# An attention step, a token sum and a first sum, each put at another place in a one-core kernel

## The chip, the cores and the metric

The kernel runs on one core of a Trainium2 chip. The metric is the time of one execution in microseconds (us), as the device measures it. The kernel before takes 810.32 us, the median of 3 runs (808.83 to 812.44).

The engines are named as in the profile: PE is TensorE (matmuls; PEld its weight loads), DVE is VectorE, ACT is ScalarE, POOL is GpSimd, and SP is SyncE, which issues most of the DMA transfers. Each works off its own queue in order. PE writes to PSUM, in banks that VectorE and ScalarE read out.

## The reference

Three layers follow each other. First an attention over 4 batches, 8 heads, 576 positions and 64 columns a head, in which the first four heads see a band of 32 positions and the others every fourth of 128:

```
scores = where(mask, scale * q @ k.T, -1e9)
attn   = softmax(scores)            # with 1e-9 added to the sum
x      = heads side by side of attn @ v      # 2304 tokens x 512
h = x @ w_in;  x2 = (h * sigmoid(h)) @ w_out         # 512 -> 2048 -> 512
a = x2 @ w1;  b = x2 @ w2;  out = ((a * b) @ w3) @ w_out2   # 512 -> 1024 -> 1024 -> 512
```

All is float32. The kernel splits each float32 factor into a high and a low part and does three matmuls for one (high x high, low x high, high x low).

## The kernel before, in words

The order of the work on each engine is written out by hand, under a manual schedule: code that is called earlier stands earlier in the queues of the engines it uses. Waits between engines come of themselves, from who reads and writes which buffer.

The 2304 tokens go through the second layer in five chunks; chunks 0, 1, 3 and 4 have 512 tokens, chunk 2 has 256. Attention for later chunks is done between the matmuls of earlier ones. A *slot* (c, f) belongs to chunk c and to the block f of 128 of the 2048 inner columns. In it PE does `h` for the next slot (12 matmuls) and `x` for this one (12 matmuls); ScalarE and VectorE turn h into g (`t`: tanh and a VectorE product, `g`: the high part on ScalarE and the low part on VectorE).

A slot's text in `SLOT` (L72) says what stands where: `h`, `H` are the halves of h, `x`, `X` those of x, `t` and `g` as above, `a` is the next attention step, and `p` is a token sum, if one is waiting. There is one text for a first slot of a pair and one for a second; `att.half()` picks it.

The attention goes two units at a time. A round has eight steps, as `ATT` (L71) lists them: V S (attention times v of the last round, scores of the next; PE), M (maxima, VectorE), E and E (exponentials, ScalarE), then in the second half N (sums on VectorE, products on GpSimd) with O (the output's high part on ScalarE and low part on VectorE), L (loads) with O, T (transposes on PE) and W (evacuation by ScalarE). T and V and S share two PSUM banks. In chunk 1 the rounds begin to lag behind the slot pairs: the limit on O holds a round back in slots 13 and 14.

The last two chunks do h by seven products of blocks in place of eight (`h_product`, L862, called in the loop at L1303). *Token sums* prepare the right-hand blocks: sums of the tokens' columns (`t_ops`), 6 early ones (x_a, x_b and a difference), 22 late ones (T1, T2, T4) and 4 last ones (T3). The late ones need tiles in the place of the attention's, so they start when the attention ends.

For the seven products there are eight rounds p. In round 0 the products go in the order 0, 2, 4, 1, 3, 5, 6, each into one of four banks in turn, and the two halves of x for the last slot of chunk 2 stand behind products 0 and 2. `collect_h` reads the banks: s1, u2, u3 and c22 hold the running sums, each finished one gets its tanh, product, high and low part. Between them, `sets` gives out single operations that prepare the third layer's weights (`set_ops`): a load of raw words, their conversion, sums and stores.

Of the kernel before, what the change touches and what calls it, by code (L numbers as in the profile page):

```python
# [9 lines left out]
F32R = mybir.dt.float32r  # L10
# [7 lines left out]
P = 128  # L18
# [53 lines left out]
SLOT = (  # L72
    ("ahapHppaxptapgX", "ahappHpxaptaXpg"),
    ("ahaHtapxgpaX", "ahHpaxtgpXaap"),
)
LATE_MICROS = 7
SET_AT = (1, 3, 6)
# [12 lines left out]
def tile_kernel(  # L90
# [338 lines left out]
    class Convert:  # L429
# [7 lines left out]
        def add(self, key, src, dst):  # L437
            self.todo.append((key, src, dst))
            return len(self.todo) - 1

        def load(self, i):
            if i < len(self.todo) and i not in self.raw:
                t = rawp.tile([P, 512, 2], I32, tag="raw", name=f"raw_{self.todo[i][0]}")
                nc.sync.dma_start(
                    out=t.rearrange("p n w -> p (n w)"), in_=self.todo[i][1].bitcast(I32)
                )
                self.raw[i] = t
# [406 lines left out]
    def load_sw(p, u):  # L854
        if p < NP and u == 0:
            dst = f32(wf[p + NP])[:, :1024].rearrange("p (s n) -> p s n", s=2)[:, :, :256]
            nc.sync.dma_start(out=dst, in_=swd[p][:, 0].rearrange("p (s k) -> p s k", s=2))
        elif p < NP:
            sw[u] = sp.tile([P, 512], F32R, tag=f"sw{u}", name=f"sw_{p}_{u}")
            nc.sync.dma_start(out=f32(sw[u]), in_=swd[p][:, u])  # L860
# [30 lines left out]
    def set_ops(s, t, raw, o):  # L891

        y = {}

        def load(k, i):
            if k < SETS:
                src = (w1, w2)[k % 2]
                nc.sync.dma_start(out=raw.rearrange("p n w -> p (n w)"), in_=src[k // 2 + i * NG // 2].bitcast(I32))

        def rebias(i):  # L900
            h = raw[:, :, 1].bitcast(F32)
            nc.scalar.activation(h, h, AF.Prelu, scale=2.0 ** -112, alpha=2.0 ** 32)

        def bits(i, x):
            if x == 0:
                y[i] = yp.tile([P, 512], I32, tag="y", name=f"ys_{s}_{i}")
                nc.vector.tensor_single_scalar(y[i], raw[:, :, 1], 3, op=ALU.logical_shift_left)
            else:
                nc.vector.scalar_tensor_tensor(
                    y[i], raw[:, :, 0], 29, y[i], op0=ALU.logical_shift_right, op1=ALU.bitwise_or  # L910
                )
                load(s + i, 1 - i)

        def half(i, k):
            return f32(y[i])[:, 256 * k:256 * k + 256]

        def total(u):
            if u == 0:
                nc.vector.tensor_add(t, half(1, 0), half(1, 1))
            elif u == 1:  # L920
                nc.vector.tensor_sub(t, t, half(0, 0))
            elif u == 3:
                nc.vector.tensor_sub(t, half(0, 1), t)
            else:
                nc.vector.tensor_sub(t, half(0, 0), half(1, 0))

        def high(k, x):
            nc.scalar.activation(o[:, k, 0].bitcast(F32R), x, AF.Copy)

        def low(k, x, at):  # L930
            nc.vector.tensor_sub(o[:, k, 1].bitcast(F32R), x, o[:, k, 0])
            nc.sync.dma_start(out=setd[s][:, at], in_=o[:, k].rearrange("p s k -> p (s k)"))

        def both(k, x, at):
            return [lambda: high(k % 2, x()), lambda: low(k % 2, x(), at)]

        def piece(i):
            return [lambda: rebias(i), lambda: bits(i, 0), lambda: bits(i, 1)]

        q = [lambda: load(0, 0)] if s == 0 else []  # L940
        q += piece(0)
        for h in range(2):
            q += both(h, lambda h=h: half(0, h), 4 + h)
        q += piece(1)
        for k, u in enumerate((0, 1, 3, 2)):
            q += [lambda u=u: total(u)] + both(k, lambda: t, u)
        return q + both(0, lambda: half(1, 1), 6)
# [187 lines left out]
    with tc.manual_schedule():  # L1135
# [49 lines left out]

        for i, (c, f) in list(enumerate(slots))[NF:-1]:
            nxt = slots[i + 1]
            for x in SLOT[c - 1][att.half()]:
                if x == "h":
                    if nxt[1] == 0:  # L1190
                        att.need(2)
                    h_part(*nxt, 0)
                elif x == "H":
                    h_part(*nxt, 1)
                    if nxt[1] == NF - 1:
                        att.limit = (c + 3) * PER_B
                elif x == "t":
                    g_tanh(*nxt)
                    g_mul(*nxt)
                elif x == "g":  # L1200
                    g_high(*nxt)
                    g_low(*nxt)
                elif x in "xX":
                    x2_part(c, f, "xX".index(x))
                    if x == "X" and f == NF - 1:
                        x2_store(c, (0, 2))
                elif x == "a":
                    if att.step() or c < 2:
                        pass
                    elif "T" in tmps:  # L1210
                        if todo:
                            todo.pop(0)()
                    else:
                        attn.close()
                        parts_ = ctx.enter_context(ExitStack())
                        sp = parts_.enter_context(tc.tile_pool(name="sp", bufs=1, side="right", reuse_waits="tile"))
                        tmps["T"] = [sp.tile([P, 2, 2, 512], F32R, tag=f"T{n}", name=f"T{n}") for n in range(2)]
                        for u in (1, 2, 3):
                            load_sw(0, u)
                        todo += late  # L1220
                elif x == "p" and todo and (len(todo) > len(early) or c == 2 and (att.out >= 3 * PER_B + 6 or "T" in tmps)):
                    todo.pop(0)()
        load_sw(0, 0)
# [3 lines left out]
        def gate(c):  # L1227
            nc.scalar.activation(ts[0], c, AF.Tanh, scale=0.5)
            return ts[0]

        def mul(c, t):
            nc.vector.scalar_tensor_tensor(c, t, 1.0, c, op0=ALU.add, op1=ALU.mult)
# [16 lines left out]
        def collect_h(p, i):  # L1249
# [29 lines left out]
            else:  # L1279
# [4 lines left out]
                split_high(ga[e], u3)  # L1284
                cs["t"] = gate(u2)

        def finish_h(p):
            u2, u3, e = cs["u2"], cs["u3"], p + NP
            mul(u2, cs["t"])
            split_low(ga[e], u3)  # L1290
            split_high(g_late(p), u2)
            split_low(g_late(p), u2)
# [10 lines left out]
        for p in range(NP):  # L1303
            if p == 1:
                bank = [ps_x.tile([P, 512], F32, tag="x", name=f"hx{k}") for k in range(4)]
                xps[3] = [(ps_h if m < 2 else ps_a).tile([P, 512], F32, tag="h" if m < 2 else "a", name=f"x2_3_{m}")
                          for m in range(KT)]
            for j, i in enumerate((0, 2, 4, 1, 3, 5, 6) if p == 0 else range(7)):
                live[i] = bank[done[0] % 4]
                done[0] += 1  # L1310
                h_product(p, i, live[i])
                if p == 0 and j < 2:
                    x2_part(2, NF - 1, j)
                    if j == 1:
                        x2_store(2, (0, 2))
                        raws = [rawp.tile([P, 2, 512], F32, tag="raw", name=f"c_{k}") for k in range(2)]
                        cs.update(s1=raws[0][:, 0], u2=raws[0][:, 1], u3=raws[1][:, 0], c22=raws[1][:, 1])
                        o = rawp.tile([P, 2, 2, 256], F32, tag="raw", name="set_out")
                        w = rawp.tile([P, 512, 2], I32, tag="raw", name="set_raw")
                        t = sp.tile([P, 256], F32, tag="set_t", name="set_t")  # L1320
                        sets = [op for s in range(SETS) for op in set_ops(s, t, w, o)]
                        ts.append(gp.tile([P, 512], F32, tag="t", name="t_s", bufs=1))
                        collect_h(0, 0)
                elif p == 0:
                    for k in {1: (1, 2), 3: (3, 4), 5: (5,), 6: (6,)}.get(i, ()):
                        collect_h(0, k)
                else:
                    collect_h(p, i)
                x_some(3, xs, 4 if i < 3 else 3, NF - 1)
                for _ in range(2 if i in (1, 2, 3, 5) else 1):  # L1330
                    if sets and (p or j > 2):
                        sets.pop(0)()
            xs = first_x(p)
        finish_h(NP - 1)
# [165 lines left out]
```

## Time and profile before

| | |
|---|---|
| median of 3 runs | 810.32 us (808.83 to 812.44) |
| the profiled execution | 808.31 us, span 806.5 us |
| PE busy | 787.4 us, 98% of the span |
| VectorE, ScalarE, GpSimd busy | 557.4, 346.6, 57.5 us |
| attention within chunks 0 to 2 | until 288 us |
| seven products | 309 to 431 us |

How to read it: the span is the time between the first and the last instruction that the profiler saw, and the profiled execution's own time is 1.8 us longer. Busy times of engines add up to more than the span, as they work side by side. Idle time counts where nobody else could have gone on: with PE at 98% that is PE's own idle time. The granted clock is given as a part of TensorE's full 2.4 GHz.

### The profile page before, as it was taken

How to read it: one execution, taken by the hardware profiler on the slowest of the kernel's cores; microseconds unless marked ns; L12 is line 12 of the kernel's file. 1: busy time of each engine (PE TensorE's matmuls, PEld its weight loads, DVE VectorE, ACT ScalarE, POOL GpSimd, SP SyncE). 2: the span in 40 equal slices, each digit the busy share in tenths (PEclk: the TensorE clock that was granted, in tenths of full speed). 3: DMA queues.
4: the chain of work that ended last, by engine and by line, in shares of the span. 5: the costliest groups of instructions: out<-in, count | busy, mean ns of one | idle time of the engine just before them, and what ended most of it. 6: DMA issues, size and time to landing. Idle time of an engine off the chain costs nothing. (4 is left out here: it accounts for less than half of the span.)

```text
span 806.5 us, 13326 instructions
## 1 busy us (share of the span) xinstructions
PE 787.4 (98%) x4829; PEld 680.7 (84%) x4829; DVE 557.4 (69%) x1333; ACT 346.6 (43%) x867; POOL 57.5 (7%) x90
## 2 busy tenths in 40 slices
PE   8999999999998899999999999999999999999997
PEld 7788888888887898788888888889999999999996
DVE  6989983867664564788884857778877655774444
ACT  7778873545444543444442625342333111321111
POOL 5101100101001100000000000013200000000000
PEclk9999999999999999999999999999999999999999
DMA  9788640533334103445532859627621760046202
GB/s 257 231 261 261 195 134 2 193 134 128 119 108 153 52 17 92 144 143 170 157 117 82 301 191 366 222 79 266 274 100 32 230 239 23 1 145 208 92 1 78
DMA packets 54561, 120.93 MB, mean 150 GB/s; under 512 B 5088, under 2 KB 25312, under 8 KB 52448
## 3 DMA queue, kind: packets, MB, share of 16 engines
q1 hardware_dynamic: 54208, 119.85, 44.3%
q8 instruction: 38, 0.62, 0.3%
q14 instruction: 27, 0.22, 0.1%
q10 hardware_dynamic: 288, 0.23, 0.1%
HBM read 87.56 MB, written 32.51 MB: 149 GB/s over the span
## 5 line engine op out<-in xcount | busy, mean ns | idle before, releaser
L1043 PE MATMUL bank<-xT,wf 128*128 128x384 f32 x864 | 163.7, 335 | 0.5 <-DVE wf L492 0.4
L1043 PEld LDWEIGHTS bank<-xT,wf 128*128 128x128 f32 x864 | 151.8, 188 | 7.2 <-DVE wf L492 0.9
L750 PE MATMUL x<-g,wf 128*128 128x512 f32 (+1 forms) x576 | 122.1, 357 | 0.7 <-ACT g L733 0.7
L710 PE MATMUL h<-xT,wf 128*128 128x512 f32 (+1 forms) x576 | 122.2, 361 | 0.0
L1099 PE MATMUL o<-wf,wf 128*128 128x512 f32 x429 | 110.0, 393 | 0.0
L710 PEld LDWEIGHTS h<-xT,wf 128*128 128x128 f32 x576 | 96.3, 192 | 15.7
L750 PEld LDWEIGHTS x<-g,wf 128*128 128x128 f32 x576 | 95.2, 189 | 16.2 <-ACT g L733 0.9
L1099 PEld LDWEIGHTS o<-wf,wf 128*128 128x128 f32 x429 | 79.5, 188 | 12.7
L1079 ACT ACTIVATE wf<-c 128x384 fp32r<-128x384 f32 x48 | 25.2, 525 | 84.0 <-DVE c L1077 83.8
L728 DVE SCALAR_TENSOR_TENSOR t<-t,h 128x512 f32<-128x512 f32 (+1 forms) x48 | 28.6, 597 | 42.4 <-ACT t L724 42.0
L1061 ACT ACTIVATE s<-bank 128x384 f32<-128x384 f32 x24 | 11.8, 492 | 103.4 <-PE bank L1043 92.8
L884 PE MATMUL x<-ga,wf 128*128 128x512 f32 x192 | 52.9, 396 | 1.9 <-DVE c L1280 1.9
L264 ACT ACTIVATE sm<-sm,nm 128x96 f32<-128x96 f32 x108 | 39.1, 365 | 23.6 <-DVE nm L254 23.5
L689 PE MATMUL wp<-wf,wf 128*128 128x512 f32 x192 | 46.7, 392 | 0.0
L884 PEld LDWEIGHTS x<-ga,wf 128*128 128x128 f32 x192 | 36.5, 191 | 10.5 <-DVE c L1280 2.3
L279 POOL TENSOR_TENSOR sm<-sm,rs 128x288 f32<-128x288 f32 x36 | 27.6, 779 | 229.8 <-DVE rs L274 63.9
L884 PE MATMUL x<-wf 128*128 128x512 f32 x192 | 43.7, 389 | 0.0
L1068 DVE TENSOR_TENSOR c<-u,bank 128x384 f32<-128x384 f32 x36 | 19.9, 552 | 32.8 <-PE bank L1043 32.6
L884 PEld LDWEIGHTS x<-wf 128*128 128x128 f32 x192 | 36.0, 188 | 7.5
L724 ACT ACTIVATE t<-h 128x512 f32<-128x512 f32 (+1 forms) x48 | 25.1, 522 | 39.0 <-PE h L710 35.6
L689 PEld LDWEIGHTS wp<-wf,wf 128*128 128x128 f32 x192 | 35.7, 188 | 7.2 <-DVE wf L605 0.4
L738 DVE TENSOR_TENSOR g<-t,g 128x512 fp32r<-128x512 f32 (+1 forms) x48 | 30.0, 626 | 15.6 <-ACT g L733 15.2
(167 smaller groups left out, 1215.1 us busy)
## 6 DMA issues: line engine op xcount, KB each, us to landing
rawj<-in_w_dram SPq DMA_DIRECT2D x26, 512.0 KB, 5.9
wf<-setd SPq DMA_DIRECT2D x11, 1024.0 KB, 5.4
wf<-setd SPq DMA_DIRECT2D x11, 768.0 KB, 7.2
raw_i<-in_w_in_dram SPq DMA_DIRECT2D x16, 512.0 KB, 4.6
raw_u<-in_w_out_dram SPq DMA_DIRECT2D x16, 512.0 KB, 4.4
swd<-sw SPq DMA_DIRECT2D x16, 512.0 KB, 2.6
sw<-swd SPq DMA_DIRECT2D x24, 256.0 KB, 3.2
setd<-set_out SPq DMA_DIRECT2D x21, 256.0 KB, 2.1
```

What stands on the lines that cost most here:

```text
L264: nc.scalar.activation(sm[:, j], sm[:, j], AF.Exp, bias=nm[:, j:j + 1], scale=-1.0, accum_out=su[:, j:j + 1],)
L279: nc.gpsimd.tensor_tensor(sm, sm, rs[:, :NB].to_broadcast([P, NB, KB]), op=ALU.mult)
L689: nc.tensor.matmul(wp_ps[i], a[:, i // 2, sa, i % 2 * P:(i % 2 + 1) * P], o[:, sb], start=(jt == 0 and x == 0), stop=(jt == NG - 1 and x = ...
L710: nc.tensor.matmul(ps, win(f, sa, kt), xT[:, kt, sb, r0:r0 + n], start=(kt == 0 and x == 0), stop=(kt == KT - 1 and x == 2),)
L724: nc.scalar.activation(gt[c, f], hps[c, f][:, :n], AF.Tanh, scale=0.5)
L728: nc.vector.scalar_tensor_tensor(t, t, 1.0, ps, op0=ALU.add, op1=ALU.mult)
L738: nc.vector.tensor_sub(g[:, 1], t, f32(g[:, 0]))
L750: nc.tensor.matmul(xps[c][m][:, :n], wout(f, sa, m), g[:, sb], start=(f == 0 and sa == 0 and sb == 0), stop=(f == NF - 1 and sb == 1),)
L884: nc.tensor.matmul(xps[c][m], wout(f, sa, m), g[:, sb], start=(first_ and sa == 0 and sb == 0), stop=(last and sb == 1),)
L1043: nc.tensor.matmul(b, a_op(s, a, sa, kt), b_op(x, sb, kt), start=(n == 0), stop=(n == 5),)
L1079: behind.append((count[0] + 1, lambda: nc.scalar.activation(hi, c[k], AF.Copy)))
L1099: nc.tensor.matmul(ps, g_block(jj, n, sa)[:, m % 3 * P:(m % 3 + 1) * P], wp_v(f, sb)[:, c0:c1], start=((first_ or len(parts) == 2) and x = ...
```

## The change

There are three edits.

One: at a slot's start the half is noted, and an `a` does a step only if the next step belongs to that half. A slot pair that has fallen out of step with the rounds then stays where it is until its half comes.

Two: once the attention has no steps left, tiles for the late token sums are taken at a slot's start, and a third text in `SLOT` is used, the same for both halves: five `p`, none of them between `t` and `g`.

Three: in round 0 of the seven products the sums are built in another order (`begin_h`): u2 = b0 + b4 and s1 = b0 + b2 after product 4, then u3 = b0 + b1 and u2 += b1, then c22 = u2 + b3 and u3 += b3, where s1 and u3 start as two copies of b0. No operation of a set is given out in round 0 any more, but the first load of raw words is issued there at once; later rounds give out 12 operations in place of 11.

```diff
 SLOT = (
     ("ahapHppaxptapgX", "ahappHpxaptaXpg"),
     ("ahaHtapxgpaX", "ahHpaxtgpXaap"),
+    ("phpHtxgpXpp",) * 2,
 )
...
-        q = [lambda: load(0, 0)] if s == 0 else []
-        q += piece(0)
+        if s == 0:
+            load(0, 0)
+        q = piece(0)
...
-            for x in SLOT[c - 1][att.half()]:
+            half = att.half()
+            if att.at == len(att.steps) and "T" not in tmps:
+                attn.close()
+                parts_ = ctx.enter_context(ExitStack())
...
+                for u in (1, 2, 3):
+                    load_sw(0, u)
+                todo += late
+            for x in SLOT[2 if "T" in tmps else c - 1][half]:
...
                 elif x == "a":
-                    if att.step() or c < 2:
-                        pass
-                    elif "T" in tmps:
-                        if todo:
-                            todo.pop(0)()
-                    else:
...
-                        todo += late
+                    if att.half() == half:
+                        att.step()
...
+        def begin_h(i):
+
+            b, s1, u2, u3, c22 = live, cs["s1"], cs["u2"], cs["u3"], cs["c22"]
+            if i == 4:
+                add(u2, s1, b[4])
+                add(s1, s1, b[2])
+                cs["t"] = gate(s1)
+            elif i == 1:
+                add(u3, u3, b[1])
+                add(u2, u2, b[1])
+                mul(s1, cs["t"])
+                ga[0] = gp.tile([P, 2, 512], F32R, tag="g", name="ga_0")
+                split_high(ga[0], s1)
+            elif i == 3:
+                add(c22, u2, b[3])
+                add(u3, u3, b[3])
+                split_low(ga[0], s1)
+                cs["t"] = gate(c22)
+            else:
+                collect_h(0, i)
...
-                        collect_h(0, 0)
+                        for k in ("s1", "u3"):
+                            nc.scalar.activation(cs[k], live[0], AF.Copy)
                 elif p == 0:
-                    for k in {1: (1, 2), 3: (3, 4), 5: (5,), 6: (6,)}.get(i, ()):
-                        collect_h(0, k)
+                    begin_h(i)
...
-                for _ in range(2 if i in (1, 2, 3, 5) else 1):
-                    if sets and (p or j > 2):
+                for _ in range(2 if i in (1, 2, 3, 5, 6) else 1):
+                    if sets and p:
                         sets.pop(0)()
```

How this moves instructions is seen at three places. The first is PE around slot (2, 1): before, the transposes t stand ahead of h_2 and a slot ahead of the o (V, then S) that need them.

```order
L750 MATMUL x_2_3_3176<-g_0_3136,wf_96 128x256
L290 MATMUL t_3202<-ident,sm_3110 96x128 x3
L290 MATMUL t_3206<-ident,sm_3115 96x128 x3
L710 MATMUL h_2_3210<-xT,wf_98 128x256 x12
L750 MATMUL x_2_0_3173<-g_1_3183,wf_97 128x256 x2
```

After, the same place has h_2 behind x, and the transposes directly ahead of V and S (`o` from `at`, and `o` from `qk`):

```order
L751 MATMUL x_2_3_3162<-g_1_3169,wf_97 128x256
L291 MATMUL t_3233<-ident,sm_3136 96x128 x3
L291 MATMUL t_3237<-ident,sm_3141 96x128 x3
L315 MATMUL o_3245<-at_3241,v_3024 64x64 x6
L315 MATMUL o_3252<-at_3243,v_3029 64x64 x6
L235 MATMUL o_3245<-qk_3026 64x96 x6
L235 MATMUL o_3252<-qk_3026 64x96 x6
L711 MATMUL h_3_3271<-xT,wf_99 128x256 x12
```

The transposes have moved behind one h and one x, and nothing is left between them and V.

The second place is VectorE in the last slots of chunk 2. Before, late sums (x_c, x_d, x_a, T) stand between the two steps t and g of tiles 10 to 12, and none around tiles 13 to 15:

```order
L831 TENSOR_TENSOR x_d<-x_d,x_a 128x512 x2
L728 SCALAR_TENSOR_TENSOR t_12_3812<-t_12_3812,h_12_3798 128x256
L831 TENSOR_TENSOR x_c<-x_c,x_b 128x512 x2
L738 TENSOR_TENSOR g_12_3823<-t_12_3812,g_12_3823 128x256
L841 TENSOR_TENSOR xT<-x_d,xT 128x512 x2
L728 SCALAR_TENSOR_TENSOR t_13_3847<-t_13_3847,h_13_3834 128x256
L738 TENSOR_TENSOR g_13_3856<-t_13_3847,g_13_3856 128x256
```

After, the same sums stand two tiles later, ahead of t and behind g:

```order
L842 TENSOR_TENSOR T_3741<-x_a,T_3741 128x512 x2
L832 TENSOR_TENSOR x_d<-x_d,x_a 128x512 x2
L729 SCALAR_TENSOR_TENSOR t_14_3873<-t_14_3873,h_14_3859 128x256
L739 TENSOR_TENSOR g_14_3882<-t_14_3873,g_14_3882 128x256
L832 TENSOR_TENSOR x_c<-x_c,x_b 128x512 x2
L842 TENSOR_TENSOR xT<-x_d,xT 128x512 x2
L729 SCALAR_TENSOR_TENSOR t_15_3909<-t_15_3909,h_15_3895 128x256
```

The sums have moved from tile 12 to tile 15.

The third place is VectorE in round 0 of the seven products, from the first sum on; hb_3932, 3933, 3934 and 3935 are the four banks (of products 0 and 3, 2 and 5, 4 and 6, and 1). Before:

```order
L1260 TENSOR_TENSOR c_3968<-c_3968,hb_3935 128x512
L1262 TENSOR_TENSOR c_3968<-c_3968,hb_3933 128x512
L1265 TENSOR_TENSOR c_3969<-c_3968,hb_3932 128x512
L1232 SCALAR_TENSOR_TENSOR c_3968<-t_s,c_3968 128x512
L1270 TENSOR_TENSOR c_3969<-c_3969,hb_3934 128x512
L1271 TENSOR_TENSOR c_3968<-c_3968,hb_3934 128x512
L1238 TENSOR_TENSOR ga_4005<-c_3968,ga_4005 128x512
L907 TENSOR_SCALAR ys_0_4011<-set_raw 128x512
```

After:

```order
L1291 TENSOR_TENSOR c_3968<-c_3968,hb_3934 128x512
L1292 TENSOR_TENSOR c_3968<-c_3968,hb_3933 128x512
L1295 TENSOR_TENSOR c_3969<-c_3969,hb_3935 128x512
L1296 TENSOR_TENSOR c_3968<-c_3968,hb_3935 128x512
L1232 SCALAR_TENSOR_TENSOR c_3968<-t_s,c_3968 128x512
L1301 TENSOR_TENSOR c_3969<-c_3968,hb_3932 128x512
L1302 TENSOR_TENSOR c_3969<-c_3969,hb_3932 128x512
L1238 TENSOR_TENSOR ga_3998<-c_3968,ga_3998 128x512
```

The sum with bank 3934 has moved from the fifth place to the first, there is one sum more, and the set's first operation is gone from the round.

## Rows read from the trace of the kernel before

**Rows 1.** PE's waits: waiting line, who ended them, us in total, times, longest.

```profile
PE t L290 <- POOL sm L279: 5.9, 7, 1.9
PE x L884 <- DVE c L1280: 1.9, 1, 1.9
PE x L750 <- ACT g L733: 0.7, 1, 0.7
PE t L290 <- ACT at L301: 0.7, 1, 0.7
```

**Rows 2.** Timeline of PE, chunk 2: start, duration, operation, count, idle before.

```profile
251.24 2.83 PE L710 MATMUL h<-xT,wf 128*128 128x256 f32 x12
...
255.42 0.92 PE L314 MATMUL o<-at,v 96*64 96x64 f32 x24
256.27 1.21 PE L234 MATMUL o<-qk 64*64 64x96 f32 x24
257.41 1.70 PE L710 MATMUL h<-xT,wf 128*128 128x256 f32 x12
...
261.61 0.53 PE L290 MATMUL t<-ident,sm 128*96 128x128 f32 x3 [1.06 <-POOL sm L279]
262.41 0.53 PE L290 MATMUL t<-ident,sm 128*96 128x128 f32 x3 [0.27 <-POOL sm L279]
262.70 1.68 PE L710 MATMUL h<-xT,wf 128*128 128x256 f32 x12
264.22 1.60 PE L750 MATMUL x<-g,wf 128*128 128x256 f32 x12
```

**Rows 3.** Timeline of the other engines in the same round of the attention.

```profile
260.89 1.47 POOL L279 TENSOR_TENSOR sm<-sm,rs 128x288 f32<-128x288 f32 x2 [10.23 <-ACT g L733]
...
262.18 0.49 ACT L301 ACTIVATE at<-t 96x384 f32<-96x384 f32 x1 [1.08 <-PE t L290]
...
264.84 0.42 DVE L728 SCALAR_TENSOR_TENSOR t<-t,h 128x256 f32<-128x256 f32 x1 [1.93 <-ACT t L724]
265.29 0.42 ACT L733 ACTIVATE g<-t 128x256 fp32r<-128x256 f32 x1 [0.49 <-DVE t L728]
```

**Rows 4.** Windows of 2 us: span, busy PE, PEld, DVE, ACT, POOL, granted clock, DMA.

```profile
252.00:254.00 2.00, 2.00 (x12) 2.00 (x11) 0.00 (x0) 0.11 (x1) 0.00 (x0) 0.54 0.81 287
...
272.00:274.00 2.00, 1.33 (x11) 1.11 (x12) 2.00 (x4) 0.81 (x2) 0.95 (x1) 1.00 0.00 0
```

**Rows 5.** Timeline of VectorE and PE at the late token sums.

```profile
300.95 1.29 DVE L831 TENSOR_TENSOR x_c<-x_c,x_b 128x512 f32<-128x512 f32 x2
...
301.54 1.83 PE L750 MATMUL x<-g,wf 128*128 128x256 f32 x12 [0.72 <-ACT g L733]
...
306.14 1.60 PE L710 MATMUL h<-xT,wf 128*128 128x256 f32 x12
```

**Rows 6.** Timeline of PE, products of rounds 0, 1 and 2.

```profile
309.02 1.55 PE L875 MATMUL hb<-xT,wf 128*128 128x512 f32 x6
310.41 0.88 PE L750 MATMUL x<-g,wf 128*128 128x256 f32 x6
...
321.86 1.52 PE L875 MATMUL hx<-xT,wf 128*128 128x512 f32 x6
...
332.48 1.57 PE L875 MATMUL hx<-xT,sw 128*128 128x512 f32 x6
...
340.79 1.54 PE L875 MATMUL hx<-xT,wf 128*128 128x512 f32 x6
...
347.68 1.56 PE L875 MATMUL hx<-xT,sw 128*128 128x512 f32 x6
```

**Rows 7.** Timeline of VectorE and ScalarE in round 0: first add, first set operation.

```profile
316.25 0.69 DVE L1260 TENSOR_TENSOR c<-c,hb 128x512 f32<-128x512 f32 x1 [2.31 <-PE hb L875]
...
321.23 0.65 ACT L902 ACTIVATE set_raw<-set_raw 128x512 f32<-128x512 f32 x1 [2.85 <-DMA set_raw<-in_w_dram]
```

**Rows 8.** DMA issues from 314 to 323 us: queue, count, size, us to landing.

```profile
set_raw<-in_w_dram SPq DMA_DIRECT2D x1, 512.0 KB, 4.6
```

More of the change, by code (lines that the diff above doesn't have):

```diff
@@ L1187, in tile_kernel @@
             nxt = slots[i + 1]
-            for x in SLOT[c - 1][att.half()]:
+            half = att.half()
+            if att.at == len(att.steps) and "T" not in tmps:
+                attn.close()
+                parts_ = ctx.enter_context(ExitStack())
+                sp = parts_.enter_context(tc.tile_pool(name="sp", bufs=1, side="right", reuse_waits="tile"))
+                tmps["T"] = [sp.tile([P, 2, 2, 512], F32R, tag=f"T{n}", name=f"T{n}") for n in range(2)]
+                for u in (1, 2, 3):
+                    load_sw(0, u)
+                todo += late
+            for x in SLOT[2 if "T" in tmps else c - 1][half]:
                 if x == "h":
@@ L1207, in tile_kernel @@
                 elif x == "a":
-                    if att.step() or c < 2:
-                        pass
-                    elif "T" in tmps:
-                        if todo:
-                            todo.pop(0)()
-                    else:
[L1214 to L1219, printed above, removed]
-                        todo += late
+                    if att.half() == half:
+                        att.step()
                 elif x == "p" and todo and (len(todo) > len(early) or c == 2 and (att.out >= 3 * PER_B + 6 or "T" in tmps)):
```

## The prediction

> **What bounds the kernel now.** I read the page's busy times first, then PE's waits, then windows of 2 us over the stretches in which PE waits, and last the timelines there. PE is busy for 787.4 of 806.5 us, so a change that leaves the matmuls as they are can only win back idle time of PE (19 us) and time in which PE runs at its lower clock. The reader is to see in the waits that this idle time has few owners [rows 1]: the transposes T of the attention wait for GpSimd's normalisation (5.9 us in 7 waits) and once for ScalarE (0.7), one x of the short chunk waits for its g (0.7), and the first x after the seven products waits for a VectorE sum (1.9). All of these lie between 248 and 329 us. The waits of the first 30 us belong to code that is not touched. Behind each of the two longest waits, 1.9 us each, the matmuls are slow for a while: h takes 2.83 us at 251.24 and 1.68 at 262.70 [rows 2], with a granted clock of 0.54 [rows 4], that is 1.2 GHz for most of the stretch.
>
> **Part 1, the attention steps.** In chunk 2 a pair of slots holds one round: V V S S, then T T, and twice h and x. Before, T comes one h and one x after S, and V one h and one x after T. From S at 256.27 the chain of scores, maxima, exponentials, sums and GpSimd's two products lasts until 262.41, 6.1 us, when the second T can start [rows 2, 3]; the PE work between takes about 4.2, and T waits 1.3 of it, in each round. The change puts both h and x of the pair between S and T: 1.14 + 2 x (1.52 + 1.5) = 7.2 us [rows 2]. On ScalarE a tanh and a g (0.42 [rows 3]) now stand ahead of the second unit's exponentials, which makes the chain at most 0.8 longer, 6.9. So T finds its input ready, with 0.3 to spare.
>
> What is late next is V, which now follows T with nothing between. ScalarE's evacuation starts 0.57 after T (261.61 to 262.18) and takes 0.49 [rows 2, 3]; the two T fill 0.6 of these 1.1 us. So V waits 0.5 at least, and all of it counts, since S, h and x stand behind V in PE's queue. ScalarE's queue has the second slot's g ahead of the evacuation, which goes 0.45 after its VectorE product [rows 3], and that product stands behind the sums and the low parts of the outputs; I take 0.7. In one of the four rounds three of the six early token sums (0.65 each [rows 5]) stand ahead of those VectorE steps; GpSimd's products there come later too, and I take 1.5. Sum: 3 x 0.7 + 1.5 = 3.6 of waits for 6.6 before: 3.0 gained. Bounds: four times 0.5 (4.6 gained), and the 6.6 that T waited (nothing gained).
>
> The clock: with no wait as long as 1.9 I expect no fall at 250, which gives back 2.83 - 1.68 = 1.2 us [rows 2]. In a later round PE is busy for only 1.33 of 2.00 us, and its granted clock stays 1.00 [rows 4]. The Trainium skill's page "TensorE: Matmul & The Clock Gate" (A second HAM failure mode: psum-queue depth-cycling) says that short idles between groups of matmuls, if there are many, make the clock swing. By that rule the four V waits, each beside small matmuls, would each be followed by a slow stretch; the window just named does not bear it out, and the rule stays a rival below.
>
> **Part 2, own slots for the token sums.** Before, 22 late operations (16 on VectorE) fill slots 8 to 11 of chunk 2, some of them between the two VectorE steps of a tile, and slots 12 to 14 are left to catch up; one x waits 0.7 at 301.54 [rows 5]. After, they start in slot 10 and last until slot 14, four or five a slot, none between the two steps of a tile. VectorE from the first sum on: 16 x 0.61 (two take 1.29, and overlap a little [rows 5]) = 9.7; three tiles at 0.45 + 0.45 + 0.34 (step, ScalarE's g, second step [rows 3]) = 3.7; about 0.5 where a tanh stands behind a ScalarE copy that itself waits for a sum; and 0.9 for the last tile: 14.8. They begin 3.3 after slot 10 starts, so the last g is there at 18.1. PE, at 2.88 a slot (306.14 to 309.02 [rows 5, 6]), would want it after five slots and one product, at 5 x 2.88 + 1.39 = 15.8. So the x wait 2.2 in all, spread over slots 13 to 15, in place of 0.7: 1.5 lost. Bounds: nothing lost (VectorE works ahead as it does before), and 3.0 lost (each tile's step waits for all five sums).
>
> **Part 3, the order of the first sums.** Before, the collection of the first round lags: the first VectorE add starts at 316.25, after four products, and ScalarE stands until 321.23 in front of the first piece of a set [rows 7], whose load takes 4.6 us to land [rows 8]; the copies and tanh of the round queue behind it. Measured on PE: from the first product to the first of the second round 12.84 us (309.02 to 321.86), while seven products at 1.39 and two half x at 0.76 make 11.25; from there to the fourth product 10.62 us (321.86 to 332.48), where the next round takes 6.89 (340.79 to 347.68) [rows 6]. Lost: 1.6 + 3.7 = 5.3 us, the slow clock behind the 1.9 us wait within it.
>
> After, the first add needs only products 0 and 4, and stands one product earlier; the bank of product 2 is read out by the second add and that of product 4 by the first. By 1.39 a product and 0.76 a half x from 309.02, product 4 ends at 314.7, and two adds of 0.69 [rows 7] behind it end at 316.2; product 5, which overwrites the bank of product 2, starts at 317.5, and product 6 at 318.9. The round has one add more (0.7 on VectorE) and one copy more (0.6 on ScalarE); both lie beside the products. No piece of a set stands in the first round any more, so the sum for which x waited 1.9 us [rows 1] comes, counted on at 0.6 to 0.7 an add, at about 322; the second round starts at 320.3, and the x that needs this sum stands two products and six x behind that, at 324.4. All 5.3 us go. If that cover failed, each add late by one product would cost up to 1.4. The first piece's load moves ahead of two loads of weights in SyncE's queue; one of these is released by product 1 at 316.1 and wanted by the second round's second product at 322.6. With 4.6 us for the piece and as much for the weights behind it they could be 2.7 late (316.1 + 4.6 + 4.6 = 325.3). Since the piece can now go out when the stores of x2 have been issued, before product 4 ends, I take 0. From the second round on the sets have 12 operations a round instead of 11; PE waits for nothing there before [rows 1]; I take 0, and 1 us as the upper bound.
>
> **Sum.** 3.0 + 1.2 - 1.5 + 5.3 = 8.0 us. The profiled execution took 808.31, 2.0 less than the median of the runs, 810.32; I take the 8.0 off the median: 802.3.
>
> **Rivals.**
> First, the sums cost nothing and V waits only for its evacuation: 4.6 + 1.2 + 5.3 = 11.1, 799.2 us. For it: VectorE worked ahead before with as many sums. Against it: before there were three empty slots to catch up in. 0.15.
> Second, the attention part moves its wait and does not shorten it, so that it doesn't do what it says: V waits as long as T did, and the clock falls as before. Left are 5.3 - 1.5 = 3.8: 806.5. For it: the loop from S over T to V and the next S is a closed chain. Against it: T's wait was in that chain with 3 us of h and x after it that now stand before it. 0.10.
> Third, the clock falls behind each V wait, four times 1.2: 3.0 + 1.2 - 4.8 - 1.5 + 5.3 = 3.2, 807.1. The skill's rule above speaks for it, the clock of 1.00 [rows 4] against it. 0.12.
> Fourth, the weights of the second round come 2.7 late and the clock falls behind that wait (3.7 - 1.9 = 1.8 was lost so before): 8.0 - 2.7 - 1.8 = 3.5, 806.8. The queue is quiet before the piece, which speaks against it. 0.06.
> Fifth, slower: the exponentials of the second unit, now behind tanh and g on ScalarE, pass the 7.2 us, so that T waits as before (6.6 in all) and V waits 1.1 each time on top, in one gap with it, behind which the clock falls in all four rounds: -4.4 + 1.2 - 4.8 - 1.5 + 5.3 = -4.2, 814.5. It decides as soon as the chain is over 1 us longer than the 6.9 I count. 0.05.
>
> **How the numbers follow.** My forecast has 0.52. Its own range is 799.5 to 805. The range for 8 in 10 reaches down to the near side of the first rival's bounds and up over the second to fourth: 798 to 807.5. About 0.5%, 4 us, is what a measurement here tells from no change. The forecast and the first rival are faster by more (0.67); of the second to fourth (0.28, gains of 3.2 to 3.8, each uncertain by 2) I count 0.11 as faster and 0.17 as no change; the fifth is slower: 0.78, 0.17, 0.05.
>
> **What would show it.** Part 1: T without waits, four waits of V for ScalarE of 0.5 to 1.5, the granted clock 1.00 from 240 to 300. Part 2: waits of x for g of about 2 us in all, the longest at tile 14. Part 3: the seven products of the first round and the x behind them without a wait, 18 us from the first product to the fourth of the second round instead of 23.5. The forecast is wrong if T still waits, if a V wait passes 1.9 us, if the x wait 4 us or more, or if PE waits between 330 and 440 us.

## The result and the profile after

The changed kernel takes 799.82 us, the median of 4 runs (798.38 to 800.78), against 810.35 in the same comparison (808.83 to 812.44): a ratio of 0.9867, with a 95% interval of 0.9839 to 0.9895. That is 10.5 us less, where 8.0 were forecast (802.3, in a range of 799.5 to 805). The profiled execution took 800.56 us with a span of 798.8; PE is busy for 784.3 us of it (98%), VectorE 557.8, ScalarE 346.0 and GpSimd 55.8.

Two stretches hold all the waits that the three edits were to remove, and they can be read in every trace below. The first goes from h of slot (2, 1) to the first of the seven products, the second from there to the fourth product of the second round. The first begins here in the trace of before, on PE (start, duration, operation):

```profile
244.97 1.60 PE L710 MATMUL h<-xT,wf 128*128 128x256 f32 x12
```

and here in the trace of after, with the other two ends behind it:

```profile
246.73 1.70 PE L711 MATMUL h<-xT,wf 128*128 128x256 f32 x12
...
304.19 1.55 PE L876 MATMUL hb<-xT,wf 128*128 128x512 f32 x6
...
316.87 1.55 PE L876 MATMUL hx<-xT,wf 128*128 128x512 f32 x6
...
323.78 1.56 PE L876 MATMUL hx<-xT,sw 128*128 128x512 f32 x6
```

With [rows 6] the first stretch was 309.02 - 244.97 = 64.05 us and is 304.19 - 246.73 = 57.46; the second was 23.46 and is 19.59. Together 10.46 us are gained. The two profiled executions differ by only 7.75, since this one came 1.8 us later to the first stretch (in the first 30 us PE waits 3.9 for loads here and not at all for loads in the other, partly in place of other waits) and took 1.0 longer behind the second (0.35 of it one wait at 494, behind a late load; the rest is not accounted for). Over the twelve traces of this study the time ahead of the first stretch differs by up to 2.8 us and the time behind the second by up to 2.6, without an order that follows the edits. A second profile of the same kernel, taken with the experiments, has 57.47 and 19.58 in a span of 795.7: the two stretches repeat to 0.01 us, and so they, not the spans, are compared from here on.

PE's waits after 240 us (line waiting, who ended it, us in total, times, longest) answer to [rows 1]:

```profile
PE x L751 <- ACT g L734: 1.5, 2, 1.0
PE o L315 <- ACT at L302: 1.2, 4, 0.4
PE t L291 <- POOL sm L280: 0.5, 1, 0.5
PE hb L876 <- ACT c L1345: 0.4, 1, 0.4
PE bank L1045 <- DVE wf L493: 0.4, 1, 0.4
PE wp L690 <- ACT wf L602: 0.3, 1, 0.3
```

The T waits of 6.6 us and the 1.9 of x for a VectorE sum are gone, and with them two waits of products 5 and 6 of round 0 for such sums (0.18 and 0.99 in the trace of before), which [rows 1] does not list. In their place stand four short waits of V (o for at), one T wait of 0.5, two x waits for g of 1.5 together, where one of 0.7 stood, and a product that waits 0.4 for a copy.

**The attention round.** T, V and S in chunk 2, with ScalarE and GpSimd beside them, where [rows 2, 3] had T behind GpSimd:

```profile
251.14 1.60 PE L751 MATMUL x<-g,wf 128*128 128x256 f32 x12
...
252.22 0.67 POOL L280 TENSOR_TENSOR sm<-sm,rs 128x288 f32<-128x288 f32 x1 [0.41 <-DVE rs L275]
...
252.58 0.89 PE L291 MATMUL t<-ident,sm 128*96 128x128 f32 x6
252.91 0.42 ACT L734 ACTIVATE g<-t 128x256 fp32r<-128x256 f32 x1 [0.92 <-DVE t L729]
253.24 0.85 ACT L302 ACTIVATE at<-t 96x384 f32<-96x384 f32 x2
...
253.76 0.95 PE L315 MATMUL o<-at,v 96*64 96x64 f32 x24 [0.29 <-ACT at L302]
```

T starts as soon as x lets it, both T run as one group of 0.89, and V waits 0.29 for the evacuation. That T does not wait is closer than it looks. In the next round the chain from S to the second product of GpSimd is this:

```profile
254.64 1.21 PE L235 MATMUL o<-qk 64*64 64x96 f32 x24
...
261.25 0.67 POOL L280 TENSOR_TENSOR sm<-sm,rs 128x288 f32<-128x288 f32 x1 [0.40 <-DVE rs L275]
```

It ends at 261.92, 7.28 us after S, though spans on GpSimd are rough in a profile. T starts at 261.63, so that its second half, 0.30 later, is due at 261.93: there is nothing to spare.

In the trace of before, the x ahead of the T of [rows 2] stands here:

```profile
258.95 1.60 PE L750 MATMUL x<-g,wf 128*128 128x256 f32 x12
```

From the start of that x to what follows T (h at 262.70) 3.75 us passed; from x at 251.14 to V at 253.76 it is 2.62. Without any wait it would be about 2.04: 1.44 for x, as between h and x without a wait, and 0.30 for each T, as from T at 262.41 to h. So the wait of T cost 1.71 a round, where the trace shows 1.06 + 0.27 = 1.33 of idle time, and V's costs 0.58, where it shows 0.29. The difference is the overlap of a group's tail with the next group, which is lost where a wait follows: x lasts 1.60 and T 0.53 where the next group starts 1.44 and 0.30 behind them, and the ends of matmuls are modelled in a profile, so that starts are the safer measure.

The window of 2 us around T and V (columns as in [rows 4]):

```profile
252.00:254.00 2.00, 1.71 (x21) 1.34 (x21) 1.31 (x5) 1.09 (x3) 0.67 (x1) 1.00 0.67 257
```

The granted clock is 1.00 where it was 0.54 [rows 4]. The one round in which T still waits has token sums on VectorE, beside which GpSimd's two products take 1.74 us:

```profile
269.82 1.74 POOL L280 TENSOR_TENSOR sm<-sm,rs 128x288 f32<-128x288 f32 x2 [7.90 <-ACT xT L334]
...
270.08 0.96 DVE L832 TENSOR_TENSOR x_a<-x_b,x_a 128x512 f32<-128x512 f32 x1
...
271.62 0.53 PE L291 MATMUL t<-ident,sm 128*96 128x128 f32 x3 [0.47 <-POOL sm L280]
```

**The late sums** (VectorE, ScalarE and PE at tile 14, answering to [rows 5]):

```profile
297.64 0.41 DVE L729 SCALAR_TENSOR_TENSOR t<-t,h 128x256 f32<-128x256 f32 x1
...
298.88 1.28 DVE L842 TENSOR_TENSOR T<-x_a,T 128x512 fp32r<-128x512 f32 x2
300.09 1.28 DVE L832 TENSOR_TENSOR x_d<-x_d,x_a 128x512 f32<-128x512 f32 x2
...
301.74 0.42 DVE L729 SCALAR_TENSOR_TENSOR t<-t,h 128x256 f32<-128x256 f32 x1 [0.37 <-ACT t L725]
302.19 0.42 ACT L734 ACTIVATE g<-t 128x256 fp32r<-128x256 f32 x1 [0.49 <-DVE t L729]
...
302.66 1.69 PE L751 MATMUL x<-g,wf 128*128 128x256 f32 x12 [0.96 <-ACT g L734]
```

From one tile's step to the next VectorE takes 4.1 us here, 297.64 to 301.74, with four sums between them; 0.37 of it is a wait for a tanh that stands behind ScalarE's copy of a sum. PE takes 2.88 a slot. Slot 10 begins here on PE:

```profile
288.28 1.60 PE L711 MATMUL h<-xT,wf 128*128 128x256 f32 x12
```

**Round 0** (SPq is SyncE's DMA queue; [rows 6 to 8] before):

```profile
306.31 0.98 PE L751 MATMUL x<-g,wf 128*128 128x256 f32 x6 [0.57 <-ACT g L734]
...
309.61 0.61 ACT L1345 ACTIVATE c<-hb 128x512 f32<-128x512 f32 x1
309.68 0.88 SPq L767 DMA_DIRECT2D x2d<-x2s  x2
...
310.89 0.69 DVE L1291 TENSOR_TENSOR c<-c,hb 128x512 f32<-128x512 f32 x1 [0.95 <-PE hb L876]
...
311.94 0.60 ACT L1345 ACTIVATE c<-hb 128x512 f32<-128x512 f32 x1 [1.72 <-DMA x2d<-x2s]
...
312.59 1.66 PE L876 MATMUL hb<-xT,sw 128*128 128x512 f32 x6 [0.44 <-ACT c L1345]
```

The second copy of b0 stands 1.72 us behind the first, since u3's tile lies in a buffer from which the store of x2 is still reading; product 3 overwrites b0's bank, and waits 0.44 for that copy. Behind it no product and no x waits.

### The profile page after: what moved, and what is told of

It reads as the page before. It is cut to its first block, busy times and chain, and to the rows that moved or that the text cites. A ratio compares the mean times of both kernels' runs of the same rounds, so it can differ in the third digit from the quotient of the medians.

```text
span 798.8 us, 13328 instructions
## 1 busy us (share of the span) xinstructions
PE 784.3 (98%) x4829; PEld 678.5 (85%) x4829; DVE 557.8 (70%) x1334; ACT 346.0 (43%) x868; POOL 55.8 (7%) x90
## 5 line engine op out<-in xcount | busy, mean ns | idle before, releaser
L711 PEld LDWEIGHTS h<-xT,wf 128*128 128x128 f32 x576 | 95.1, 189 | 15.8
```

The source lines that it names most:

```text
L711: nc.tensor.matmul(ps, win(f, sa, kt), xT[:, kt, sb, r0:r0 + n], start=(kt == 0 and x == 0), stop=(kt == KT - 1 and x == 2),)
```

## The experiments

Each kernel is the changed kernel with one edit more, unless the text says otherwise. The table gives the two stretches from each trace and the median of all runs. e1, e2, e3 and e6 shared a chip and a comparison (before: 808.66), so did e0, e11, e4 and e5 (809.05), and e7 and e12 (809.94).

| kernel | first stretch | second | both | median, us |
|---|---|---|---|---|
| before | 64.05 | 23.46 | 87.51 | 810.35 |
| after | 57.46 | 19.59 | 77.05 | 799.82 |
| e1, steps untied | 65.20 | 18.74 | 83.94 | 805.53 |
| e2, old slot text | 57.40 | 18.71 | 76.11 | 797.26 |
| e3, round 0 as before | 57.49 | 22.38 | 79.87 | 802.50 |
| e6, early end | 58.25 | 18.73 | 76.98 | 799.12 |
| e0, after again | 57.47 | 19.58 | 77.05 | 798.87 |
| e11, four places, early end, own copy | 55.96 | 18.03 | 73.99 | 795.88 |
| e4, old order, sets out | 57.48 | 20.51 | 77.99 | 800.00 |
| e5, new order, sets in | 57.49 | 23.05 | 80.54 | 802.53 |
| e7, own copy | 57.50 | 18.85 | 76.35 | 798.88 |
| e12, four places | 55.97 | 19.05 | 75.02 | 797.50 |

**e1: the attention steps untied.**

```diff
                 elif x == "a":
-                    if att.half() == half:
-                        att.step()
+                    att.step()
```

> The changed kernel with one edit undone: an attention step is done at every a, whichever half it was meant for. The third slot text and the order of the first sums stay. Theory (the tie to the half gave the gain of 6.6 us between h of slot (2, 1) and the first product): T waits for GpSimd again, 5 to 6 us in all with the longest near 1.9, the granted clock falls at 250, that stretch takes about 63 us in place of 57.5, and the time is 805 to 806.5 us. Rival (the own slots of the token sums gave it, since VectorE is freer): the stretch stays within 1 us of 57.5, the time 799 to 801.

Measured: 805.53 us (803.42 to 808.26, 10 runs), 0.9967 of before with an interval of 0.9944 to 0.9989. T's waits came back to the digit:

```profile
PE t L291 <- POOL sm L280: 5.9, 7, 1.9
PE x L751 <- ACT g L734: 1.5, 2, 1.0
...
PE t L291 <- ACT at L302: 0.7, 1, 0.7
```

and behind the longest of them h is slow again, as at 251.24 in [rows 2]:

```profile
249.35 0.53 PE L291 MATMUL t<-ident,sm 128*96 128x128 f32 x3 [1.91 <-POOL sm L280]
250.16 0.87 PE L291 MATMUL t<-ident,sm 128*96 128x128 f32 x3 [0.27 <-POOL sm L280]
250.69 2.85 PE L711 MATMUL h<-xT,wf 128*128 128x256 f32 x12
```

The theory holds and the rival falls: edit one is worth 83.94 - 77.05 = 6.9 us. The first stretch came out 2 us longer than the expected 63, partly as both x waits now lie in it; over both stretches the 6.9 are close to the theory's 6.6.

**e2: the third slot text taken out.**

```diff
-            for x in SLOT[2 if "T" in tmps else c - 1][half]:
+            for x in SLOT[c - 1][half]:
...
                 elif x == "a":
-                    if att.half() == half:
+                    if "T" in tmps:
+                        if todo:
+                            todo.pop(0)()
+                    elif att.half() == half:
                         att.step()
```

> The changed kernel with the third slot text taken out: the late token sums stand where they stood before in a slot of chunk 2 (six places, some between the two VectorE steps of a tile); the attention steps stay tied to their half and the order of the first sums stays. Theory (the sums are hidden beside PE by either text): x waits for g 1 to 2.5 us in all against 1.5, the time within 1 us of the changed kernel, 799 to 801. Rival (a sum between t and g delays each tile's g, so that the text matters): x waits 3.5 us or more in slots 12 to 15 and the time is 802 to 804.

Measured: 797.26 us (796.66 to 797.75), 0.9858 of before (0.9812 to 0.9905). Only one x wait is left:

```profile
297.11 1.83 PE L751 MATMUL x<-g,wf 128*128 128x256 f32 x12 [0.52 <-ACT g L734]
```

The rival falls. So does the expectation of 1 to 2.5 us of waits, and the time lies below the expected 799: by the stretches the old text is 0.9 us better (76.11 against 77.05), and the time agrees, within what the runs can tell. The sums between a tile's two steps did no harm, the first stretch being 57.40 against 57.46; in the second the last tile's x no longer waits. Edit two is a small loss.

**e3, e4, e5: round 0.** e3 takes back all of edit three, e4 the order of the sums alone, e5 the absence of the sets alone.

```diff
e3, e4:
-                        for k in ("s1", "u3"):
-                            nc.scalar.activation(cs[k], live[0], AF.Copy)
+                        collect_h(0, 0)
...
-                    begin_h(i)
+                    for k in {1: (1, 2), 3: (3, 4), 5: (5,), 6: (6,)}.get(i, ()):
+                        collect_h(0, k)
e3, e5:
-        if s == 0:
-            load(0, 0)
-        q = piece(0)
+        q = [lambda: load(0, 0)] if s == 0 else []
+        q += piece(0)
...
-                for _ in range(2 if i in (1, 2, 3, 5, 6) else 1):
-                    if sets and p:
+                for _ in range(2 if i in (1, 2, 3, 5) else 1):
+                    if sets and (p or j > 2):
```

> The changed kernel with the third edit undone whole: in round 0 of the seven products the sums are built in the old order, and the sets' operations are given out in round 0 as before. Theory (the edit gave 3.9 us there): from the first product to the fourth of the second round 23 to 24 us in place of 19.6, x waits about 1.9 us for a VectorE sum, the clock falls behind it, time 803 to 805. Rival (the earlier attention end frees VectorE and ScalarE so that the old order would do as well): 20.5 us or less there, time 800 to 801.

> The changed kernel with the old order of the sums in round 0, the sets' operations still kept out of that round. Theory (the set's first piece, for which ScalarE stood, is most of the third edit): 20 to 21 us from the first product to the fourth of the second round, against 19.6 of the changed kernel and 22.4 with the edit undone whole, time 0.5 to 1.5 us above the changed kernel. Rival (the order of the sums is most of it): 21.8 us or more, since the sixth and seventh products still wait 1.2 us for the sums that free their banks and x still waits over 1 us, time 2 to 3 us above.

> The changed kernel with the new order of the sums in round 0, but the sets' operations given out there as before. Theory (the set's first piece is most of the third edit): 21.5 to 22.5 us from the first product to the fourth of the second round, with a wait of x for a VectorE sum of 1 us or more, time 2 to 3 us above the changed kernel. Rival (the order of the sums is most of it): 20.5 us or less, time within 1 us of the changed kernel.

Measured: e3 802.50 us (0.9916, 0.989 to 0.9942), e4 800.00 (0.9888, 0.9846 to 0.993), e5 802.53 (0.9908, 0.9872 to 0.9944). In the second stretch, against the 19.58 of e0, the old order costs 0.93 with the sets out, the sets cost 3.47 with the new order, and both together 2.80. e4 kept to its theory (20.5 us, no x wait), though with the two bank waits that its rival named; e3 lay a little under its 23 us and its 803, its clock did not fall, and e5 lay a little over its 22.5. In e5 ScalarE stands for the raw words, then x waits, then h is slow:

```profile
315.83 0.68 ACT L903 ACTIVATE set_raw<-set_raw 128x512 f32<-128x512 f32 x1 [2.54 <-DMA set_raw<-in_w_dram]
...
321.54 1.22 PE L885 MATMUL x<-ga,wf 128*128 128x512 f32 x2 [2.46 <-DVE c L1279]
322.56 2.41 PE L876 MATMUL hx<-xT,wf 128*128 128x512 f32 x6
```

with this window of the clock in e5:

```profile
322.00:324.00 2.00, 2.00 (x6) 1.52 (x6) 1.39 (x4) 1.88 (x4) 0.00 (x0) 0.50 0.76 212
```

In e3 the same x waits less, and what follows is not slow:

```profile
322.58 0.73 PE L885 MATMUL x<-ga,wf 128*128 128x512 f32 x2 [1.57 <-DVE c L1279]
323.15 1.53 PE L876 MATMUL hx<-xT,wf 128*128 128x512 f32 x6
```

So the new order alone would have won nothing (23.05 against e3's 22.38): keeping the sets' first piece out of the round is what won, and the order adds 0.9 to it. That x waits longer in e5 than in e3 can be read in the two traces: counted from the first product, the sum comes at 18.1 in e5 and 18.8 in e3, but PE is there at 16.4 and 18.0, since only in e3 do products 5 and 6 wait (0.18 and 0.98) for their banks. e5 also differs in one thing that was not meant: its second copy of b0 does not wait for the store of x2, and product 3 does not wait either.

```profile
308.09 1.10 ACT L1344 ACTIVATE c<-hb 128x512 f32<-128x512 f32 x2
```

By the price that e7 gives this wait below, 0.74, the sets cost more than the 3.47, about 4.2 by that estimate.

**e6: the attention may end in either half,** so that the sums start one slot earlier.

```diff
-                    if att.half() == half:
+                    if att.half() == half or att.at >= len(att.steps) - 2:
                         att.step()
```

> The changed kernel, but the last two attention steps may be done in either half, so that the attention ends one slot earlier and the late token sums start one slot earlier. Theory (the x waits of 1.5 us in slots 13 to 15 are there because the sums start too late by less than one slot's worth): x waits for g fall to 0.3 us or less, the stretch from h of slot (2, 1) to the first product is about 56 us in place of 57.5, time 797.5 to 798.8. Rival (the longer x wait is from the scheduling of ScalarE's g behind its own token copies, wherever the sums start): x waits stay above 1 us and the time is that of the changed kernel, 799.3 to 800.5.

Measured: 799.12 us (796.51 to 800.45), 0.9875 (0.9832 to 0.9919). My theory fell: the x waits are the same two, one tile earlier.

```profile
296.98 1.70 PE L751 MATMUL x<-g,wf 128*128 128x256 f32 x12 [0.97 <-ACT g L734]
...
300.63 1.70 PE L751 MATMUL x<-g,wf 128*128 128x256 f32 x12 [0.51 <-ACT g L734]
```

Both stretches together are 76.98 against 77.05. The time lies just under the rival's 799.3, and its x waits are there, but its reason, ScalarE's copies, is not shown by this. The start did not matter, and what VectorE has to do a slot accounts for that, as it falls behind while the sums last: four sums a slot at 0.61, two steps of 0.42, and 0.45 idle between them make 3.7 us against PE's 2.88. e11 tests this account against it.

**e11, e12 and e7: fewer sums a slot, and the copy elsewhere.** e12 changes the third text, e7 the copy of b0, and e11 does both and e6's edit.

```diff
e11, e12:
-    ("phpHtxgpXpp",) * 2,
+    ("phHtpxgXpp",) * 2,
e11, e7:
-                add(u3, u3, b[1])
+                add(u3, cs["b0"], b[1])
...
-                        for k in ("s1", "u3"):
+                        cs["b0"] = yp.tile([P, 512], I32, tag="y", name="b0").bitcast(F32)
+                        for k in ("s1", "b0"):
```

> The changed kernel with two more steps. The third slot text has four places instead of five, one of them between the two VectorE steps of a tile, and the attention may end in either half, so that six slots hold the late sums; and the second copy of b0 in round 0 goes to a tile of its own instead of u3's, whose buffer waits for the store of x2. Theory (the x waits come from VectorE's load while the sums last: four sums of 0.61 us, two steps and an idle 0.45 a slot are 3.8 us against PE's 2.88, and a start one slot earlier alone cannot mend that; with three sums a slot, one in the idle time, the load is about 2.8): x waits for g fall from 1.5 us to 0.3 or less, the third product's wait of 0.44 for the copy goes, and the time is 1.5 to 2 us below the changed kernel's on the same chip, about 797.8. Rival (the tanh behind a ScalarE copy that waits for a sum sets them): x waits stay at 1 us or more, and only 0.44 is gained.

> The changed kernel itself, on the same chip as the kernels beside it. Expected by all theories: 799 to 800.5 us; V waits for ScalarE 4 times about 0.3 us; x waits for g 1.5 us in all; 19.6 us from the first product to the fourth of the second round.

> The changed kernel with the third slot text of four places alone, one of them between the two VectorE steps of a tile; the late sums start where they do in the changed kernel, so that four VectorE sums more are left behind the last slot. Theory (VectorE's load a slot while the sums last makes x wait): x waits for g 0.3 us or less, the wait of 0.44 for the copy of b0 stays, 19.0 to 19.2 us from the first product to the fourth of the second round if the sums left over are hidden. Rival (the start one slot earlier is needed too): the sums left over delay the first sums of round 0, products or x wait there 0.5 us or more beyond the 0.44.

> The changed kernel, with the second copy of b0 in round 0 put into a tile of its own instead of u3's, whose buffer still holds x2 until its store has read it. Theory (the store makes the third product wait): the wait of 0.44 us goes, the copies run one behind the other, and the seven products and what lies before the second round's fourth product take 19.1 to 19.2 us instead of 19.6; x waits for g stay at 1.5 us. Rival (ScalarE is late there for another reason, the copies of the last token sum ahead of it): the wait stays at 0.3 us or more.

Measured: e11 795.88 us (794.19 to 797.05), 0.9833 of before (0.9803 to 0.9863), beside the changed kernel's 798.87 (797.49 to 800.05) on the same chip, 0.9871 (0.9841 to 0.99). By its median and its stretches it is the fastest kernel of the study; it gained 3.0, where 1.5 to 2 were expected, and the stretches say the same (77.05 to 73.99). I had priced the x waits by their idle time of 1.5; start to start they cost 2.2, as worked out below. The x waits are gone. VectorE still waits 0.37 twice for a tanh behind a ScalarE copy (at 292.97 and 298.95) without a wait of PE behind it, so that the rival falls. The idle time between two steps of a tile now holds a sum:

```profile
302.01 0.41 DVE L729 SCALAR_TENSOR_TENSOR t<-t,h 128x256 f32<-128x256 f32 x1
...
302.34 0.68 DVE L842 TENSOR_TENSOR xT<-x_d,xT 128x512 fp32r<-128x512 f32 x1
302.46 0.42 ACT L734 ACTIVATE g<-t 128x256 fp32r<-128x256 f32 x1 [1.10 <-DVE t L729]
```

e12 (797.50, 2 runs) shows that the text alone removes both x waits. It changes two things at once, the number of sums a slot and the place of one. The place alone did not do it in e2, which also has sums between the steps, but mostly four or more a tile: its first stretch is 57.40 where e12's is 55.97. Whether the smaller number would do without the place was not tried. The four sums left over delay VectorE's part of x2s (0.43 behind ScalarE's, 0.12 in the changed kernel), and with it the store for which the second copy of b0 waits, so that product 3 waits longer:

```profile
308.85 1.66 PE L876 MATMUL hb<-xT,sw 128*128 128x512 f32 x6 [0.75 <-ACT c L1345]
```

0.31 us more than the changed kernel, under the 0.5 of its rival. e7 (798.88, 2 runs) has the second copy right behind the first, and product 3 without a wait:

```profile
307.10 0.60 ACT L1346 ACTIVATE c<-hb 128x512 f32<-128x512 f32 x1
307.58 0.62 ACT L1346 ACTIVATE b<-hb 128x512 f32<-128x512 f32 x1
...
309.47 1.56 PE L876 MATMUL hb<-xT,sw 128*128 128x512 f32 x6
```

The store did make it wait. Without that wait the second stretch is 0.74 us shorter (18.85 against 19.59), more than the 0.44 shown: start to start, product 3 came 1.97 behind product 1 in the changed kernel (310.62 to 312.59) and comes 1.36 behind it here.

## Why the prediction came out as it did

The direction and the three mechanisms were right, and the time lies in the stated range, near its lower end; the sum was 2.5 us short, 8.0 against 10.5. By stretch: 2.7 us forecast in the first (3.0 + 1.2 - 1.5) and 6.6 measured, 5.3 in the second and 3.9 measured. By part, worked out below, the waits of T and V gave 2.3 more than forecast, the late sums cost 0.4 less, round 0 gave 0.7 less; the 0.5 that are left are steps of PE that became shorter in the attention rounds (an h and an x that follow each other take 1.44 us; behind T and ahead of V they took 1.52 and 1.53). That the forecast is not further off is in part luck, as the 0.7 too much in part 3 offsets some of the rest.

**Part 1, the waits: the step that failed.** "3 x 0.7 + 1.5 = 3.6 of waits for 6.6 before" subtracts two prices of different kinds. The 0.7 of V was worked out start to start (evacuation 1.1 behind T, of which two T fill 0.6); the 6.6 of T was the idle time that the trace shows. Start to start, from x to what follows T, the four rounds took 4.83, 3.75, 4.12 and 3.76 us before and 2.62, 2.61, 3.29 and 2.61 after; with 2.04 for each without a wait, T's waits cost 8.3 and V's (with the one T wait left) cost 3.0. Gained are 5.3, not 3.0: 1.7 of the difference is T's price, 0.6 is V's, which was near: 0.57 to 0.58 against "0.5 at least" and the 0.7 taken, and 1.25 against 1.5 in the heavy round. There I had V wait; it is T that waits 0.47 for GpSimd and V 0.35, and by my own sign ("The forecast is wrong if T still waits") this one wait speaks against me. A second step failed without a price: T was to find its input ready "with 0.3 to spare" at the end of a chain of 6.9 us. The chain took 7.28, the way of PE to the second T 7.29; the margin was luck, and the fifth rival, in which T waits again, was nearer than I counted.

**Part 1, the clock.** As forecast: from h at 251.24 to the x behind it took 2.67 us before and 1.5 now, 1.2 gained. The third rival, a fall behind each V wait, did not happen. The granted clock is 1.00 around all four waits of 0.29 to 0.35. The Trainium skill's page "TensorE: Matmul & The Clock Gate" (A second HAM failure mode: psum-queue depth-cycling) tells of a kernel in which small idles between groups of matmuls are frequent enough to make the clock swing. This trace does not bear that out for its four waits, some 9 us apart.

**Part 2.** VectorE did what was worked out: the sums begin 3.3 us after slot 10 starts (288.28 to 291.58), and the last g ends at 306.26, 18.0 after it, where 18.1 was forecast. The last tile's x starts at 306.31; without a wait it would have been 288.28 + 15.8 = 304.1, so that 2.2 us are lost, as forecast, though the waits that the trace shows add up to 1.5. What was mis-sized is again what it replaces: the 0.72 of [rows 5] cost 1.16 from start to start (the two slots from h at 299.22 to h at 306.14 took 6.92, where two take 5.76), so that 1.1 are lost, not 1.5. Against the old text (e2) the loss is 0.9.

**Part 3.** Forecast were 18 us with no wait in the round. The sets' piece, the x behind the sums and the weights of the second round went as argued: no x waits on a sum, the second product of the second round starts without a wait, and between 330 and 440 us PE waits nowhere. Of the 1.6 us above 18, some 0.7 is the tail of the late sums (the x wait at 306.31), which part 2 had counted and had not placed here. The rest is a failed step: "one copy more (0.6 on ScalarE); both lie beside the products". The copy's destination was still being read by a store, which no view of the engines' busy time shows; e7 puts its price at 0.74. With both removed e11 measures 18.03 us, and the cost of round 0 is as forecast. That edit three is worth 2.8 by e3 and not 5.3 comes from the setting. In e3 the x wait is 1.57 where it was 1.89, and the clock does not fall behind it: from the h behind the wait to the fourth product PE takes 2.29 us, where it took 3.88 before, so that 1.6 less is lost. The store's wait of 0.74 lies on the new order's side alone; the sums' tail lies on both.

**The rivals.** By its time the first (799.2) came nearest, but its sums are not free. The fourth did not happen, and T's old pattern, which the second and fifth would have kept, shows only in e1, with the edit taken out.

## What to carry to other kernels

Price a wait from start to start, between two instructions that stand on either side of it, and compare it with the same pair where nothing waits: the idle time that a trace shows leaves out the overlap that the group before it loses, here 0.2 to 0.6 us a wait, and a sum that mixes both prices is off. When VectorE gets extra work between matmuls, count its load per slot against PE's; an earlier start did not mend a load that was too high per slot (e6), nor did sums in the idle gap of a dependent pair as long as their number stayed high (e2), and one sum there with fewer in the slot did (e12). Before counting an added copy as free, look up what last read its destination's buffer: a store that still reads it holds the copy, and with it the bank that the copy was to free.

## What the runs showed of the hardware

Four waits of PE of 1.89 to 2.46 us were each followed by matmuls at the lower clock (a group of 2.83, 2.48, 2.85 and 2.41 us where 1.5 to 1.6 is usual): before at 250 and 328, e1 at 249, e5 at 322. The wait of 1.57 us at the same place in e3 was not, nor were those of 0.96 to 1.06, nor one of 1.72 at 492 in e7, around which the granted clock is 1.00. The former are thus dearer by another 1.2 to 1.6 us, from start to start against the same groups elsewhere. GpSimd's product of 128x288 took 0.67 us alone and 1.74 for two beside a VectorE sum of two inputs, which itself took 0.96 in place of 0.68.
